# Retention and a gated feed-forward on one core: the first two batches of attention loaded with two tokens per partition and cut by head halves, the first down projection by rows

## The chip, the cores and the metric

The kernel runs on one core of a Trainium2 chip. The metric is the device time in microseconds (us) of one execution, as the median of the runs; three runs of the kernel before gave 305.97 us (305.95 to 306.12). The engines are named as the profile names them: PE (matmuls; its weight loads PEld), DVE, ACT, POOL, and SP, which here only issues DMAs. q1 is the queue of SP's DMAs.

## The reference

```
scores = q @ k^T / sqrt(64)             # 8 batches, 8 heads, 576 tokens, 64 per head
ret    = scores * gamma_h^(i - j) for i >= j, else 0      # gamma_h = 1 - 2^(-5-h)
x      = (ret @ v), heads side by side  # 4608 tokens x 512
h      = x @ w_in                       # 512 x 2048
out    = (h * sigmoid(beta * h)) @ w_out  # 2048 x 512, float32
```

The decay gamma^(i-j) is a product of a gain per query and a gain per key, so the kernel scales q by one (table gq) and v, or in one place k, by the other (table gv), and the rest is linear attention with a causal mask: within a chunk of 128 tokens the masked scores, and from earlier chunks a carried state k^T v per head.

## The kernel before

**Blocks.** 512 tokens of each batch form a block of four chunks of 128; the last 64 tokens of all eight batches form a ninth block, the tails. A block's attention gives xT (the 512 values of a token on partitions); `up` (L466) makes one of 16 slices `fo` of 128 hidden values for a block with four matmuls of 512 columns and a Silu on ACT; `down` (L499) adds the slices of a token group `ms` (a quarter of the block) into one bank and copies it out. Order of the blocks: 0 to 6, tails, 7.

**Order of the work.** Nothing is scheduled for the kernel: each engine runs its instructions in the order in which the program issues them. The opening (L540 to L589) is written out by hand: batch 0, chunk by chunk. Then `merged` (L526) walks through `fill`, the list of up and down pieces, and puts every step of `streams` whose key is at most n ahead of `fill[n]`. d0 is the index of the first down piece of block 0 in that list (16; 15 after the change, as the first half pair leaves the list), u1 that of the first up of block 1. The steps of batch 1's attention have keys from d0+7 to u1+7, so that they lie between downs of block 0 and ups of block 1.

**One chunk of batch 0 or 1.** Loads: q of a batch with four tokens per partition (runs of 1 KB, `load_q` L73), k and v by chunk with one token per partition (runs of 256 bytes, `load_kv` L85). `pre_q` and `pre` (L241, L255) scale and cast them to bf16; `t_q`, `t_k` (L297, L304) transpose on PE and copy out of PSUM on ACT or DVE; `a_sc` (L317) makes the scores of 8 heads into two banks, and DVE multiplies each with the mask (L332) into R; `a_st` (L389) adds the chunk to the state, and copies it into block-diagonal tiles sbds; `a_O` (L367) multiplies R with v, `a_cross` (L353) adds the carried state's part, `a_x` (L379) copies to xT. In the opening, 14 dummy matmuls of 128 columns (`warm_up`, L209) lie between these steps. From batch 2 on, transposes are DMAs and other functions are used (`a_O4`, `a_cross4`, `x4`).

**Weights.** w_in comes in eight pieces of 256 columns (512 KB each), cast to bf16 by POOL and DVE (L185, L188); w_out in four of 1 MB, cast and divided by beta on POOL, DVE and ACT (L200, L202, L204). All DMAs but one are issued by SP, in program order: q, k and v of batch 0, w_in, w_out, batch 1, batch 2. In up 1 the first 10 slices are made in two halves of 256 columns, chunks 0 and 1 first, so that they can start before chunks 2 and 3 are done.

PSUM has eight banks: three with the tag mm, two sc, two O, one st.

## Time and profile before

| | us |
|---|---|
| median of the runs | 305.97 |
| the profiled execution | 305.54 |
| its span | 303.8 |
| PE busy | 293.4 (97% of the span) |
| ACT, DVE, POOL busy | 134.1, 108.0, 99.9 |
| first up of block 0 (PE, L488) | 18.46 |
| first down of block 0 (PE, L506) | 32.96 |
| first up of block 1 | 51.11 |
| first down of block 1 | 68.01 |

The span is the time from the first to the last instruction in the profiled execution; the execution's own time has 1.74 us more around it. A row of an order of time gives start, length, engine, line, operation, out<-in, shapes, the count of merged instructions, and in brackets how long the engine stood before it and what released it. Matmuls overlap, so that the length of a PE row is some 0.16 us more than the distance to the next.

### The profile page before, as it was taken

To read this page: it belongs to the slowest core of one execution; us is meant where nothing else is said; L and a number is where in the kernel's file an instruction comes from. 1 tells how busy PE (TensorE), PEld (TensorE's weight loads), DVE (VectorE), ACT (ScalarE), POOL (GpSimd) and SP (SyncE) were. 2 spreads that over 40 slices of the span, in tenths; PEclk is the share of its full clock that TensorE was granted. 3 is DMA by queue.
4 is the path that set the end of the run, shared out by engine and by line. 5 is a ranking of instruction groups with operands and counts; after the bars stand their busy time and mean duration, and the time that the engine had idled before them with its cause. 6 is when DMAs were issued, how large, how long until landed. Compare 5 with 4: busy or idle time off the path is not lost.

```text
span 303.8 us, 5689 instructions
## 1 busy us (share of the span) xinstructions
PE 293.4 (97%) x2311; PEld 151.3 (50%) x2345; DVE 108.0 (36%) x202; ACT 134.1 (44%) x227; POOL 99.9 (33%) x138
## 2 busy tenths in 40 slices
PE   7799999999999999999999999999999999999995
PEld 5544456854544454445444544454455544444444
DVE  6588566504640433133222413151346510020012
ACT  5567546781147313741374127511771058107700
POOL 4666317552840723350308030942342000000000
PEclk9999999999999999999999999999999999999999
DMA  8999999999999999908982889997996110131011
GB/s 210 219 344 363 385 252 244 237 189 243 173 249 265 233 190 230 262 12 158 252 219 66 156 226 243 214 187 184 185 200 112 60 45 0 32 73 35 2 69 69
DMA packets 129210, 53.86 MB, mean 177 GB/s; under 512 B 109968, under 2 KB 122656, under 8 KB 129184
## 3 DMA queue, kind: packets, MB, share of 16 engines
q1 hardware_dynamic: 129152, 53.49, 78.4%
q8 instruction: 18, 0.29, 0.4%
q14 instruction: 8, 0.07, 0.1%
q10 hardware_dynamic: 32, 0.01, 0.0%
HBM read 36.71 MB, written 9.44 MB: 152 GB/s over the span
## 4 chain that ended last, share of the span: by engine, by line
PE 87%; DMA 6%; SPq 4%; issue 1%; POOL 1%; DVE 0%; POOLq 0%
PE po L506 41%; PE ph L473 36%; SPq L94 3%; DMA wt<-in_moe_w_out_dram 3%; PE sc L327 3%; DMA wt<-in_moe_w_in_dram 2%; PE O L441 2%; PE st L402 2%; PE O L453 1%; SPq L177 1%; POOL w_out_sb L200 1%; PE O L376 0%; PE st L405 0%; SPq L82 0%; PE T L307 0%
## 5 line engine op out<-in xcount | busy, mean ns | idle before, releaser
L475 ACT ACTIVATE gT<-ph,beta_sb 128x512 bf16<-128x512 f32 (+1 forms) x152 | 99.5, 659 | 82.2 <-PE ph L473 81.7
L506 PE MATMUL po<-w_out_sb,gT 128*128 128x512 bf16 (+2 forms) x591 | 127.1, 368 | 2.1 <-issue 1.3
L473 PE MATMUL ph<-xT,w_in_sb 128*128 128x512 bf16 (+1 forms) x592 | 125.1, 365 | 0.8 <-issue 0.2
L473 PEld LDWEIGHTS <-w_in_sb 128*128 128x128 bf16 x608 | 58.4, 98 | 63.0 <-DVE w_in_sb L188 0.9
L506 PEld LDWEIGHTS <-gT 128*128 128x128 bf16 x608 | 56.8, 98 | 63.9 <-issue 0.6
L332 DVE TENSOR_TENSOR R<-sc,causal 128x512 bf16<-128x512 f32 x72 | 45.0, 684 | 81.4 <-PE sc L327 80.3
L513 DVE COPY ot<-po 128x512 f32<-128x512 f32 (+2 forms) x34 | 22.4, 657 | 77.2 <-PE po L506 74.4
L277 POOL CAST kn<-kvn 128x512 bf16<-128x512 f32 x32 | 19.5, 612 | 55.5 <-DMA kvn<-in_k_dram 55.1
L259 POOL TENSOR_TENSOR vn<-kvn,gv 128x512 bf16<-128x512 f32 x32 | 33.3, 1042 | 13.1 <-DMA kvn<-in_v_dram 6.3
L251 POOL TENSOR_TENSOR qs<-qn,gq 128x512 bf16<-128x512 f32 x24 | 24.3, 1042 | 35.1 <-DMA qn<-in_q_dram 35.1
L408 ACT CAST sbq<-st 128x256 bf16<-128x256 f32 x18 | 6.6, 369 | 35.8 <-PE st L402 35.8
L461 DVE CAST xT<-O 128x512 bf16<-128x512 f32 x20 | 12.7, 685 | 20.2 <-PE O L453 20.2
L327 PE MATMUL sc<-qT,kT 64*128 64x128 bf16 x256 | 10.8, 218 | 0.7 <-ACT kT L308 0.6
L188 DVE CAST w_in_sb<-wt 64x256 bf16<-64x256 f32 x32 | 10.7, 334 | 1.4 <-DMA wt<-in_moe_w_in_dram 0.3
L461 ACT CAST xT<-O 128x512 bf16<-128x512 f32 x8 | 4.7, 587 | 13.4 <-PE O L453 13.4
L327 PEld LDWEIGHTS <-kT 64*128 64x128 bf16 x288 | 8.2, 94 | 3.8 <-issue 1.7
L185 POOL CAST w_in_sb<-wt 128x256 bf16<-128x256 f32 x16 | 7.2, 469 | 5.3 <-DMA wt<-in_moe_w_in_dram 5.3
L402 PEld LDWEIGHTS <-kn 128*64 128x64 bf16 x192 | 5.1, 110 | 7.6 <-issue 6.4
L212 PE MATMUL ph<-warm 128*128 128x128 f32 (+1 forms) x24 | 6.5, 405 | 1.2 <-DVE warm L119 1.2
L441 PE MATMUL O<-R,vn 128*64 128x128 bf16 x224 | 7.7, 220 | 0.0
L402 PE MATMUL st<-vn,kn 128*64 128x64 bf16 x192 | 7.4, 200 | 0.0
L266 POOL TENSOR_TENSOR kn<-tln,gq 128x512 bf16<-128x512 f32 x4 | 4.2, 1042 | 9.8 <-DMA tln<-in_q_dram 5.9
(69 smaller groups left out, 103.4 us busy)
## 6 DMA issues: line engine op xcount, KB each, us to landing
qn<-in_q_dram SPq DMA_DIRECT2D x16, 512.0 KB, 5.8
kvn<-in_k_dram SPq DMA_DIRECT2D x32, 256.0 KB, 5.1
kvn<-in_v_dram SPq DMA_DIRECT2D x32, 256.0 KB, 5.0
out_dram<-ot SPq DMA_DIRECT2D x31, 256.0 KB, 2.8
wt<-in_moe_w_out_dram SPq DMA_DIRECT2D x4, 1024.0 KB, 9.7
wt<-in_moe_w_in_dram SPq DMA_DIRECT2D x6, 512.0 KB, 8.6
out_dram<-ot SPq DMA_DIRECT2D x9, 128.0 KB, 2.4
wt<-in_moe_w_in_dram SPq DMA_DIRECT2D x4, 256.0 KB, 5.8
```

The lines of the kernel that those rows point to most:

```text
L251: e.tensor_tensor(batch[b]["qs"][:, cs, hs], q_tiles[b][:, hs, cs].rearrange("p h i d -> p i h d"), gq[:, cs, hs].unsqueeze(3).to_broadcas ...
L259: nc.gpsimd.tensor_tensor(live[i]["vn"][:], kv_tiles.pop(i)[:, 1], gains(gv, c), ALU.mult)
L277: nc.gpsimd.tensor_copy(kn[:, c % 2], t[:, 0])
L327: nc.tensor.matmul(view(sc[j][:, p, :]), L["kT"][r, p, :], rhs, start=True, stop=True, skip_group_check=True)
L332: nc.vector.tensor_tensor(R[:, j], sc[j][:], m_b, ALU.mult)
L402: nc.tensor.matmul(st[j * D:(j + 1) * D, p, :D], L["kn"][:, 2 * p + j, :], L["vn"][:, 2 * p + j, :], start=(c == 0 and p == 0), stop=True, ...
L441: nc.tensor.matmul(out4(i, p, hh), L["vn"][:, 2 * p + j, :], rhs if b is None else rhs.rearrange("k (i s) -> k i s", i=CB), start=c % 2 == ...
L461: (nc.scalar.copy if n == 1 else nc.vector.tensor_copy)(to, O.rearrange("k p i s -> k p (i s)") if b is None else O[:])
L473: nc.tensor.matmul(ph, w_in_sb[:, ko, fo * P:(fo + 1) * P], xts[m][:, ko, :, w], start=(ko == 0), stop=(ko == KO - 1))
L475: nc.scalar.activation(gts[m][:, fo, :, w], ph, ACT.Silu, scale=beta_sb[:, fo:fo + 1])
L506: nc.tensor.matmul(po[:, :nn], gT[:, fo, ms, :], w_out_sb[:, fo, n0:n0 + nn], start=(fo == 0), stop=(fo == FO - 1))
L513: (nc.scalar.copy if m == 0 else nc.vector.tensor_copy)(ot, po[:, :nn])
```

## The change

- Batches 0 and 1 are loaded in spans of 256 tokens with two neighbouring tokens on a partition, so that a run of k or v has 512 bytes (for batch 1, q too); batch 0 by halves of the heads, all keys first. A chunk is then one half of the partitions of a span.
- Batch 0 is computed by head halves. Its keys take the gain in place of its values. Scores, outputs, states and carried terms of both batches work on halves of the partitions; batch 1's carried term stays 128x128. Batch 1 adds up its states anew for each chunk from the spans. No dummy matmul stands between the opening's steps.
- The first up pair is split: its first half (xT of heads 0 to 3) stands before the xT copy of the other heads. Rows of w_in are ordered to suit (head pairs p//2 instead of p%2, also in `a_O4`, `a_cross4`, `x4`).
- Down of block 0 takes one row `fo` for all four token groups at a time; the fourth group uses the st bank. w_out is loaded in half pieces, batch 1's first span is loaded ahead of the last w_out piece, whose cast has the key d0+12. Up 1 is in halves throughout.
- Masks of later batches and the zeroes of sbds are made on POOL after w_in's casts; the safe betas are made on DVE.

The longest parts of the diff; what is not shown are the gain tables, new masks (`cuts`, one per token parity), tile shapes and the renamed halves of `up`.

```diff
+    def load_span(b, j, cc, hs):
+
+        if (b, j, cc) not in spans:
+            spans[b, j, cc] = stage.tile([P, H, 2, D], F32, name="kvn", tag="kvn", bufs=NQ)
+        nc.sync.dma_start(spans[b, j, cc][:, hs].rearrange("p h i d -> p h (i d)"),
+                          (k, v)[j][b, hs, cc * W:(cc + 1) * W, :].rearrange("h (p i) d -> p h (i d)", i=2))
...
+    for j, g in ((0, 0), (0, 1), (1, 0), (1, 1)):
+        for cc in range(2):
+            load_span(0, j, cc, both[g])
...
+        if g == 0:
+            nc.sync.dma_start(t[:, :2], w_in_r[:, :2, f0:f0 + fn])
+            for ko in (2, 3):
+                for a, b in ((0, D), (D, 0)):
+                    nc.sync.dma_start(t[a:a + D, ko], moe_w_in[ko * P + b:ko * P + b + D, f0:f0 + fn])
...
+        for ko in kos:
+            if ko < 2 or g == 0:
+                (nc.vector if ko == 3 else nc.gpsimd).tensor_copy(w_in_sb[:, ko, f0:f0 + fn], t[:, ko])
...
+        for w in range(0, KO, 2):
+            nc.sync.dma_start(t[:, w:w + 2], w_out_r[:, g * KO + w:g * KO + w + 2, :])
...
+            hs, cs, e = slice(n // 2 * HP, (n // 2 + 1) * HP), slice(n % 2 * 2, n % 2 * 2 + 2), (nc.vector, nc.gpsimd)[n % 2]
+        elif b == 1:
+            hs, cs, e = slice(n % 2 * HP, (n % 2 + 1) * HP), slice(n // 2 * 2, n // 2 * 2 + 2), nc.vector
...
+        gain = gq2 if b == 1 else gq
...
+    def pre_span(b, j, cc, hs, e, gain=False):
+
+        if (b, cc) not in pair:
+            pair[b, cc] = [sb.tile([P, 2, H, D], BF16, name="kn", tag="kn", bufs=4),
+                           sb.tile([P, 2, HP, P], BF16, name="kT", tag="kT", bufs=4),
+                           sb.tile([P, 2, H, D], BF16, name="vn", tag="vn", bufs=3)]
+        put(e, pair[b, cc][2 * j][:, :, hs], spans[b, j, cc][:, hs].rearrange("p h i d -> p i h d"),
+            gv2[:, 2 * cc:2 * cc + 2, hs].unsqueeze(3).to_broadcast([P, 2, hs.stop - hs.start, D]) if gain else None)
...
+    def t_k(b, cc, ps, tag, e):
+
+        kn, kT = pair[b, cc][:2]
+        T = psum.tile([P, 2, len(ps), P], BF16, name="T", tag=tag, bufs=BANKS[tag])
+        for i in range(2):
+            for n, p in enumerate(ps):
+                nc.tensor.transpose(T[:, i, n, :], heads(kn[:, i], p), ident[:])
+        evict(e, kT[:, :, ps[0]:ps[-1] + 1, :], T[:])
...
+    def sc_span(b, cc, g, tags):
+
+        kT = pair[b, cc][1]
+        Rs[b, cc, g] = R = sb.tile([P, 2, 2, 2, P], BF16, name="R", tag="R", bufs=4)
+        sc = [psum.tile([P, 2, 2, P], F32, name="sc", tag=tag, bufs=BANKS[tag]) for tag in tags]
+        for n, i in ((n, i) for n in range(2) for i in range(2)):
+            p = 2 * g + n
+            for j, h in ((0, 0), (1, 1), (0, 1), (1, 0)):
+                r = slice(j * D, (j + 1) * D)
+                nc.tensor.matmul(by(b, sc[j][h * D:(h + 1) * D, n, i, :]), kT[r, i, p, h * D:(h + 1) * D], q_span(b, 2 * cc + h, r, p),
+                                 start=True, stop=True, skip_group_check=True)
+        for j in range(2):
+            nc.vector.tensor_tensor(R[:, j], sc[j][:], cuts[b][:].unsqueeze(1).to_broadcast([P, 2, 2, P]), ALU.mult)
...
+    def O_span(b, cc, g):
+
+        vn, R = pair[b, cc][2], Rs[b, cc, g]
+        for n, i in ((n, i) for n in range(2) for i in range(2)):
+            p = 2 * g + n
+            for j, h in ((0, 0), (1, 1), (0, 1), (1, 0)):
+                r, hh = slice(h * D, (h + 1) * D), j ^ p // 2
+                key, o = region(b, 2 * cc + h, p)
+                nc.tensor.matmul(o[hh * D:(hh + 1) * D], vn[r, i, 2 * p + j, :], by(b, R[r, j, n, i, :]),
+                                 start=begins(key, (hh,)), stop=False, skip_group_check=True)
...
+    def cross_span(b, c, ps):
+
+        cc, h = (c - 1) // 2, (c - 1) % 2
+        for p in ps:
+            key, o = region(b, c, p)
+            if b:
+                nc.tensor.matmul(o, sbds[c - 1][:, 2 * p:2 * p + 2].rearrange("k h d -> k (h d)"),
+                                 q_span(b, c, slice(0, P), p), start=False, stop=True, skip_group_check=True)
+                continue
+            for j in range(2):
+                r, hh = slice(j * D, (j + 1) * D), j ^ p // 2
+                nc.tensor.matmul(o[hh * D:(hh + 1) * D], sbq[c - 1][r, p, :], q_span(b, c, r, p), start=False, stop=True,
+                                 skip_group_check=True)
...
+    def st_terms(b, x, ps, terms, at=0):
+
+        for p in ps:
+            for t, (d, r) in enumerate((d, r) for d, r in terms):
+                kn, _, vn = pair[b, d]
+                for i in range(2):
+                    for j in range(2):
+                        o = (*states[b], x, p, j)
+                        nc.tensor.matmul(states[b][0][j * D:(j + 1) * D, x, p, :], kn[r, i, 2 * p + j, :], vn[r, i, 2 * p + j, :],
+                                         start=begins(states[b][1], (j,)), stop=True, skip_group_check=True)
...
+    low, high, rows = slice(0, D), slice(D, P), slice(0, P)
+
+    def new_states(b, cc, tag):
+        states[b] = (psum.tile([P, 2, HP, D], F32, name="st", tag=tag, bufs=BANKS[tag]), ("st", b, cc))
+    def blocks_of(x, to, es):
+
+        for j in range(2):
+            r = slice(j * D, (j + 1) * D)
+            evict(es[j], to[r, slice(1, 7) if j else slice(0, 10)].rearrange("k (u y) d -> k u y d", u=2)[:, :, 0:3:2],
+                  states[1][0][r, x].rearrange("k (u y) d -> k u y d", u=2))
+    def st_early(b, ps, es):
+
+        st_terms(b, 0, ps, [(0, low)])
+        st_terms(b, 1, ps, [(0, rows)])
+        if b == 0:
+            evict(es[0], sbq_all[:, 0:2, ps[0]:ps[-1] + 1], states[b][0][:, :, ps[0]:ps[-1] + 1])
+        else:
+            for x in range(2):
+                blocks_of(x, sbds[x], es)
+    def st_late(b, ps, es):
+
+        st_terms(b, 1, ps, [(1, low)] if b == 0 else [(0, rows), (1, low)])
+        if b == 0:
+            evict(es[0], sbq[2][:, ps[0]:ps[-1] + 1], states[b][0][:, 1, ps[0]:ps[-1] + 1])
+        else:
+            blocks_of(1, sbds[2], es)
+    def st_end(b, e):
+
+        st_terms(b, 1, range(HP), [(1, high)])
+        evict(e, ends[b][:], states[b][0][:, 1])
+    def x_span(b, key, es):
+
+        for h, e in enumerate(es):
+            O = Os[b, key][h]
+            if b == 0:
+                evict(e, xt(b)[:, 2 * key:2 * key + 2].rearrange("k p i (c h s) -> k (p i) c h s", c=2, h=2)[:, :, :, h],
+                      O.rearrange("k p i c s -> k (p i) c s"))
+            else:
+                evict(e, xt(b)[:, :, 2 * key:2 * key + 2, h * D:(h + 1) * D], O[:])
...
-            pos_[ms] = psum.tile([P, d_model], F32, name="po", tag="mm", bufs=3)
+            tag = "st" if (m, ms) == (0, 3) else "mm"
+            pos_[ms] = psum.tile([P, d_model], F32, name="po", tag=tag, bufs=BANKS[tag])
...
+        (nc.scalar.copy if m == 0 and ms % 2 == 0 else nc.vector.tensor_copy)(ot, po[:, :nn])
...
+    V, A, Z = nc.vector, nc.scalar, nc.gpsimd
+
+    g0, g1, lo2, hi2 = both[0], both[1], (0, 1), (2, 3)
     betas()
     betas_safe()
...
+    warm_up(4)
+    pre_q(0, 0)
+    pre_q(0, 1)
+    t_q(0, 0, "mm", A)
+    pre_q(0, 2)
+    pre_q(0, 3)
+    t_q(0, 1, "mm", A)
+    pre_span(0, 0, 0, g0, V, True)
+    t_k(0, 0, lo2, "mm", V)
+    pre_span(0, 0, 1, g0, Z, True)
+    pre_span(0, 0, 0, g1, Z, True)
+    pre_span(0, 0, 1, g1, Z, True)
+    sc_span(0, 0, 0, ("sc", "sc"))
+    t_k(0, 1, lo2, "mm", A)
+    sc_span(0, 1, 0, ("O", "O"))
+    pre_span(0, 1, 0, g0, Z)
+    pre_span(0, 1, 1, g0, Z)
+    t_k(0, 0, hi2, "mm", A)
+    sc_span(0, 0, 1, ("sc", "sc"))
+    t_k(0, 1, hi2, "mm", A)
+    new_states(0, 0, "st")
+    st_early(0, lo2, (A,))
+    new_span_O(0, 0, ("O", "O"))
+    O_span(0, 0, 0)
+    sc_span(0, 1, 1, ("mm", "mm"))
+    pre_span(0, 1, 0, g1, Z)
+    pre_span(0, 1, 1, g1, Z)
+    O_span(0, 1, 0)
+    st_late(0, lo2, (A,))
+    for c in (3, 1, 2):
+        cross_span(0, c, lo2)
+    st_early(0, hi2, (A,))
+    new_span_O(0, 1, ("sc", "sc"))
+    O_span(0, 0, 1)
+    x_span(0, 0, (A, A))
+    cast_w_in(0, (0, 1))
+    O_span(0, 1, 1)
+    st_late(0, hi2, (A,))
+    for c in (3, 1, 2):
+        cross_span(0, c, hi2)
+    up_pair(0, 0, 0)
+    x_span(0, 1, (V, A))
+    cast_w_in(0, (2, 3))
     cast_w_in(1)
     nc.vector.reciprocal(rbeta_sb[:], beta_sb[:])
...
+    def masks():
+
+        nc.gpsimd.memset(causal2[:], 1.0)
+        nc.gpsimd.affine_select(out=causal2[:], in_=causal2[:], pattern=[[1, P]], compare_op=ALU.is_ge,
+                                fill=0.0, base=0, channel_multiplier=-1)
+        nc.gpsimd.memset(causal2[:TL, TL:], 0.0)
+        cut_of(1)
+        nc.gpsimd.memset(causal[:], 1.0)
+        nc.gpsimd.affine_select(out=causal[:], in_=causal[:], pattern=[[1, CB], [CB, PC]], compare_op=ALU.is_ge,
+                                fill=0.0, base=0, channel_multiplier=-1)
+        for t in sbds:
+            nc.gpsimd.memset(t[:], 0.0)
+
+    fill = [F(up_pair, 0, 0, 1)] + [F(up, 0, fo) for fo in range(2, FO)]
...
-    def down_rows(n):
-
-        for fo, ms in [(2 * n + x // 2, x % 2) for x in range(4)] if n < 2 else [(fo, 2) for fo in range(4)]:
+    def down_row(n):
+
+        for fo, ms in [(n, ms) for ms in range(4)] if n < FO - 2 else [(fo, 2 * (n - FO + 2) + x) for x in range(2) for fo in (FO - 2, FO - 1)]:
             down(0, ms, fo, 1)
 
-    fill += [F(down_rows, n) for n in range(3)]
-    fill += [F(down, 0, ms, f0) for f0 in range(4, FO, 4) for ms in range(3)]
-    fill += [F(down, 0, 3, f0) for f0 in range(0, FO, 4)]
+    fill += [F(down_row, n) for n in range(FO)]
...
     u1 = len(fill)
-    fill += [F(up, 1, fo, 2 * x, 2) for x in range(2) for fo in range(10)]
-    fill += [F(up, 1, fo) for fo in range(10, FO)]
+    NH = FO
+    fill += [F(up, 1, fo, 2 * x, 2) for x in range(2) for fo in range(NH)]
+    fill += [F(up, 1, fo) for fo in range(NH, FO)]
     fill += [F(down, 1, ms, f0) for ms in range(MB // P) for f0 in range(0, FO, 4)]
-    base = {1: u1 + 10}
...
+    def span_sc(cc, g):
+        sc_span(1, cc, g, ("O", "O") if g else ("sc", "sc"))
+
+    def span_out(cc, g):
+
+        if g == 0:
+            new_span_O(1, cc, ("sc", "sc"))
+        O_span(1, cc, g)
+
+    def span_st(cc):
+
+        new_states(1, cc, "st" if cc else "O")
+        (st_late if cc else st_early)(1, range(HP), (A, V))
+
+    def span_rest(cc):
+
+        if cc:
+            cross_span(1, 2, range(HP))
+        cross_span(1, 2 * cc + 1, range(HP))
+        x_span(1, cc, (A, V))
+
+    def kv1(cc, t):
+        return [(t, F(load_q, 1, (cc,)))] + [(t, F(load_span, 1, j, cc, all_h)) for j in range(2)]
+
+    def span_steps(cc, q0, tq, k0, tk, s0, v0, t0, o0, x0):
+
+        return [(q0, F(pre_q, 1, 2 * cc)), (q0, F(pre_q, 1, 2 * cc + 1)), (tq, F(t_q, 1, cc, "O", V)),
+                (k0, F(pre_span, 1, 0, cc, both[0], A)), (k0, F(pre_span, 1, 0, cc, both[1], Z)),
+                (tk, F(t_k, 1, cc, range(HP), "O", A)), (s0, F(span_sc, cc, 0)), (s0 + .01, F(span_sc, cc, 1)),
+                (v0, F(pre_span, 1, 1, cc, both[0], V, True)), (v0, F(pre_span, 1, 1, cc, both[1], Z, True)),
+                (t0, F(span_st, cc)), (o0, F(span_out, cc, 0)), (o0 + .01, F(span_out, cc, 1)),
+                (x0, F(span_rest, cc))]
...
+    streams = [[(0, F(st_end, 0, A)), (0, F(load_w_out, 0)), (0.1, F(cast_w_in, 2)), (2.1, F(cast_w_in, 3)), (2.2, F(load_w_out, 1)),
                 (4.1, F(cast_w_in, 4)), (6.1, F(cast_w_in, 5)), (6.2, F(load_w_out, 2)), (8.1, F(cast_w_in, 6)),
-                (10.1, F(cast_w_in, 7)), (10.2, F(load_w_out, 3))],
-               [(d0 - 4 + 3.3 * g, F(cast_w_out, g)) for g in range(WG)],
...
+                (10.1, F(cast_w_in, 7)), (10.5, F(masks))] + kv1(0, 10.15) + [(10.2, F(load_w_out, 3))] + kv1(1, 10.3),
+               [(d0 - 3 + 3 * g, F(cast_w_out, g)) for g in range(WG - 1)] + [(d0 + 12, F(cast_w_out, WG - 1))],
                [(10.4, F(load_q, 2))] + [(10.4, F(load_kv, 2 * CB + n)) for n in range(2)],
...
+               [(u1 + 5, F(load_kv, 2 * CB + 2)), (u1 + 8.1, F(x_q, XB, 0)), (u1 + 8.2, F(x_q, XB, 1)),
+                (u1 + 8.3, F(x_k, XB, 0)), (u1 + 8.5, F(load_kv, 2 * CB + 3)),
                 (base[2] - 4.5, F(release, 4)), (base[2] + 8, F(release, 4))],
...
+               [(u1 + 8, F(pre_q, XB, n)) for n in range(4)],
+               span_steps(0, d0 + 8.5, d0 + 9.5, d0 + 9.5, d0 + 10.5, d0 + 11.5, d0 + 12.5, d0 + 15.8, d0 + 15.9, u1),
+               span_steps(1, u1 + 1, u1 + 2, u1 + 3, u1 + 5, u1 + 8, u1 + 7, u1 + 11, u1 + NH - 1, u1 + NH),
+               [(u1 + NH + 2, F(st_end, 1, A))]]
```

## Prediction

> **What bounds the kernel now.** I read the busy time by stage first, then TensorE's waits, then its order of time. The columns of the first view are the stretch, its length, and busy time (count) of PE, PEld, DVE, ACT and POOL.
>
> ```profile
> 0.00:18.46 18.46, 14.08 (x149) 10.13 (x150) 11.03 (x29) 10.95 (x22) 10.21 (x26) 1.00 1.10 237
> 18.46:32.96 14.50, 14.25 (x62) 5.89 (x65) 11.74 (x35) 10.77 (x17) 8.38 (x19) 1.00 1.07 363
> 32.96:51.11 18.15, 17.89 (x135) 9.27 (x136) 10.87 (x20) 8.75 (x17) 6.25 (x8) 1.00 1.08 281
> 51.11:68.01 16.90, 16.83 (x156) 12.07 (x157) 5.38 (x10) 13.62 (x30) 10.77 (x12) 1.00 1.13 221
> 68.01:303.80 235.79, 230.35 (x1812) 113.96 (x1839) 69.00 (x110) 89.97 (x146) 64.33 (x74) 1.00 0.70 150
> ```
>
> From 18.46 us on PE is busy without a break, and the waits from 20 us to the end are nothing:
>
> ```profile
> PE po L506 <- issue: 1.3, 8, 0.2
> PE ph L473 <- issue: 0.2, 1, 0.2
> PE po L506 <- POOL w_out_sb L200: 0.2, 1, 0.2
> ```
>
> So the time is the opening (until the first up), plus PE's work, plus whatever waits a change puts in. Everything after up of batch 1 (68.01) keeps its instructions; only head pairs are regrouped there, at the same count and shape. The change is decided before 68 us. PE's order of time there:
>
> ```profile
> 18.46 0.59 PE L488 MATMUL ph<-xT,w_in_sb 128*128 128x512 bf16 x2 [0.17 <-ACT xT L386]
> 20.47 12.66 PE L473 MATMUL ph<-xT,w_in_sb 128*128 128x512 bf16 x55
> 32.96 1.55 PE L506 MATMUL po<-w_out_sb,gT 128*128 128x512 bf16 x6
> 34.66 9.22 PE L506 MATMUL po<-w_out_sb,gT 128*128 128x512 bf16 x41 [0.15 <-POOL w_out_sb L200]
> ```
>
> First up at 18.46, first down at 32.96. In the trace matmuls of 512 columns start 0.216 us apart, those of 256 0.109, those of 128 0.056.
>
> **The loads.** Each row below starts when its load lands (POOL, then DVE):
>
> ```profile
> 12.29 0.61 POOL L277 CAST kn<-kvn 128x512 bf16<-128x512 f32 x1 [0.16 <-DMA kvn<-in_k_dram]
> 13.47 0.61 POOL L277 CAST kn<-kvn 128x512 bf16<-128x512 f32 x1 [0.57 <-DMA kvn<-in_k_dram]
> 21.82 0.92 POOL L185 CAST w_in_sb<-wt 128x256 bf16<-128x256 f32 x2 [0.24 <-DMA wt<-in_moe_w_in_dram]
> 23.32 0.92 POOL L185 CAST w_in_sb<-wt 128x256 bf16<-128x256 f32 x2 [0.58 <-DMA wt<-in_moe_w_in_dram]
> 37.41 1.28 DVE L204 TENSOR_SCALAR w_out_sb<-wt,rbeta_sb 128x512 bf16<-128x512 f32 x3 [1.43 <-DMA wt<-in_moe_w_out_dram]
> 40.11 1.28 DVE L204 TENSOR_SCALAR w_out_sb<-wt,rbeta_sb 128x512 bf16<-128x512 f32 x3 [1.43 <-DMA wt<-in_moe_w_out_dram]
> ```
>
> 256 KB of keys in 256-byte runs take 1.18 us, 256 KB of w_in in 1 KB runs 0.75 (512 KB in 1.50), of w_out in 2 KB runs 0.68. Runs of 512 bytes are not in the trace: between 0.68 and 1.18; a straight line of the time per run through the first two gives 0.90, which I take. Eight loads of batch 0 then end at 6.2 (second half of q) + 7.2 = 13.4 instead of 15.8, and all weights come 2.4 us earlier. The three more issues for w_in's first piece (0.47 each on SP, by the chain of waits) lie under that backlog. (DMA: Bandwidth & Descriptors, Specifications, of the Trainium skill names 512 bytes as the smallest transfer at line rate; by that it would be 0.75 and 12.2 us. No run here shows it yet, and the opening below would gain at most 0.3 by it.)
>
> **The opening, step by step.** The safe betas move from POOL to DVE ahead of the first q product, and wait for ACT, which now has two more gain tables (0.2 each) before its table load: q products on DVE at 5.9 instead of 4.74. Two at 0.69 end at 7.2, the first key product at 7.9, transposes (0.4), DVE's copy (0.43) and scores (0.4) at 9.3. Eight mask products at 0.65 on DVE then end at 15.1, each pair also waiting for keys: POOL makes two q products and three key products at 1.04 (end 11.1), ACT copies four transposes at 0.58 (last 13.2). Behind them outputs, and on ACT in order: a state 0.4, two xT copies 0.59 (16.0 to 17.2), the last state 0.3 (17.5). PE's carried terms wait for that, so the first up pair starts at 17.95, 0.5 earlier. Its second half needs xT (18.8) and DVE's cast (19.2); st_end (0.45) lies in that wait. The long run of ups starts at 20.1 instead of 20.47 and, with weights early, runs 56 x 0.216 = 12.1 without its present 0.4 of stalls: first down at 32.2 instead of 32.96, **gain 0.8**. Ends: no gain, or 1.9 more if only loads set it. POOL's moved masks (seven memsets and four selects of 0.14 to 0.5 each by the nearest rows, 3.9 us) lie before its w_out casts at 1.26: row 1 of w_out at 33.0 against a need at 33.1, so nothing; 0.8 if they are at their upper end.
>
> **Batch 1, from first down to the end of up 1.** Before, 68.01 - 32.96 = 35.05 us, of which down 64 x 0.216 = 13.8 and up 13.9 leave 7.3 for attention. After, PE's own attention is 32 transposes 1.8; 64 scores and 64 outputs on 64x64 tiles, 0.056 per four as the trace's L453, 1.8; 12 carried terms 0.7; 80 state matmuls at 0.03 a pair as L402, 1.2; and 23 changes of tiling at 0.095 (first score of a group 0.15 behind a transpose, not 0.056), 2.2: 7.65. So +0.35. The waits are what costs:
>
> ```profile
> 47.32 2.59 DVE L332 TENSOR_TENSOR R<-sc,causal 128x512 bf16<-128x512 f32 x4 [0.94 <-PE sc L327]
> 44.41 1.02 ACT L302 COPY qT<-T 128x1024 bf16<-128x1024 bf16 x1
> 51.04 0.77 ACT L416 CAST sbd<-st 64x256 bf16<-64x256 f32 x2
> ```
>
> - **Row 12.** The cast of the last quarter of w_out is due at d0+12, just behind the scores of span 0 (d0+11.5), and just ahead of down_row(12), which reads its first row. Each engine runs in program order, so DVE does four mask products (2.59) before the cast (0.48). PE has 0.3 of scores left and then stands: 0.2 + 2.59 + 0.48 + 0.1 - 0.4 = 2.97. Today these casts are done at 41.4, long before the products at 47.3. The load is not the cause: w_out's last MB now follows 1.5 MB of batch 1 (5.4 us), lands its first half at 41.8, and PE comes to row 12 at 32.2 + 12 x 0.86 + 0.9 + 0.4 = 43.9. Ends: 2.5 and 3.7.
> - **Key copy.** Transposes at d0+11, scores one row (0.86) later, ACT's copy of 1024 columns 1.02 + 0.2: 0.4 (0 to 0.7).
> - **First half of up 1.** States, outputs, carried term and xT copies all stand at u1, directly ahead of the up that reads xT. After the carried term: 0.15 + 0.69 copy + 0.1, and ACT and DVE have last downs to copy first: 1.07 (0.5 to 1.3). Now one transpose group and a state lie in that gap.
> - **Second q.** Products (2 x 0.69) queue on DVE behind the xT copy, two half ups (0.87) hide less than they take: 0.4 (0 to 0.6).
> - **Second half.** The same shape at u1+16: 0.9 (0.5 to 1.2). Now three half ups (1.3) lie between.
>
> Sum 5.7 of waits, 0.35 of work: +6.1 (low ends 2.5 + 0.5 + 0.5 + 0.35 = 3.9); less the opening's 0.8: **+5.3**. ACT has 32 half silus at 0.43 per 0.437 of PE, and five more copies (2.9 us), but PE has 4.6 of attention there to let it catch up. SP's later transposes for batch 2 are issued behind POOL's products at some 57 us and needed after 73; PE shows no slack to absorb the delay later, nor waits that would grow. The profiled execution had a span of 303.8 and took 305.54, so 1.74 lies around it, and it was 0.43 below the median 305.97. Span 309.1, execution 310.8, on the median **311.3**.
>
> **Rivals.**
> - *The runs bring nothing* (512-byte runs at 1.18): values land at 15.7, POOL and ACT follow 1.1 later: 312.4. Chance 0.1.
> - *PE slower in the opening.* The dummy matmuls between attention steps go:
>
> ```profile
> L212 PE MATMUL ph<-warm 128*128 128x128 f32 x14 | 2.7, 297 | 0.0
> ```
>
>   The granted clock is 1.00 in every stretch above, with them. If it fell, the pair's eight matmuls (1.7) and the opening's groups in series (1.5) would take twice as long: +3.2, 314.5. Chance 0.1. (TensorE: Matmul & The Clock Gate of the Trainium skill, Part 1 and Part 4, says that an idle window halves the clock, and that transposes don't count as activity; no run here shows it.)
> - *The start follows the loads*, as now (last value 15.8, first up 18.46, 2.7 behind): 13.4 + 2.7 = 16.1, 1.9 better: 309.4. Chance 0.07.
> - *No wait at row 12*, were the cast ahead of the products: 308.3. Chance 0.06. Against it speaks the order in the code.
> - *Not slower.* The same start at the best rate: values at 6.2 + 8 x 0.68 = 11.6, first up at 14.3, 4.15 earlier and 0.4 of stalls gone: -4.55. It decides against the price of batch 1: at its central value 305.97 + 6.1 - 4.55 = 307.5, at its low ends 305.97 + 3.9 - 4.55 = 305.3. It needs these low ends and the first up before 15.0 us. DVE's and ACT's queues speak against it. Chance 0.07.
>
> **How the numbers follow.** The forecast has 0.60 and its own range, from the ends above, is 309.4 to 312.8. 0.2% (0.6 us) is about what a measurement of this kernel can tell from no change. The range 307.7 to 314.3 leaves out the last rival and part of the slower PE. Faster 0.05 and same 0.02 are the last rival; slower 0.93.
>
> **What would show it.** First up near 18.0 and first down near 32.2; key loads 0.9 apart; PE idle for about 3 us ahead of down_row(12), ended by DVE's w_out cast, with four mask products in front of it on DVE; two waits of about 1 us for xT; up 1 ending near 73.4. Wrong if PE stays busy between 32 and 73, or if the first up starts before 15.

## The result, and the profile after

The changed kernel takes **321.97 us** (median of 4 runs, 319.29 to 324.16) against 305.96 (305.95 to 306.12): ratio 1.0493, 95% interval 1.0426 to 1.0559. The slowest of the four, 324.16 us, lies over 1.5% above the fastest and is left out of the ratio. Slower, as forecast, but by 16 us where the forecast had 5.3. The profiled execution took 321.44 us with a span of 319.7. First the stages of the changed kernel, with the columns of the prediction's first table (stretch, length, busy time and count of PE, PEld, DVE, ACT, POOL; then granted clock, DMA share, GB/s):

```profile
0.00:21.23 21.23, 13.75 (x242) 10.29 (x242) 11.38 (x26) 9.56 (x20) 14.28 (x34) 0.84 1.01 285
21.23:36.45 15.22, 14.53 (x82) 6.41 (x81) 14.42 (x34) 11.12 (x17) 10.25 (x22) 1.00 1.02 337
36.45:60.52 24.07, 18.85 (x179) 9.25 (x179) 11.29 (x23) 6.57 (x12) 10.98 (x13) 0.93 1.13 274
60.52:82.94 22.42, 21.29 (x264) 16.77 (x265) 6.51 (x10) 16.11 (x36) 7.57 (x9) 0.92 0.82 154
82.94:319.70 236.76, 230.54 (x1813) 113.87 (x1839) 69.05 (x110) 90.02 (x146) 58.17 (x68) 1.00 0.61 138
```

The five stretches are longer by 2.77, 0.72, 5.92, 5.52 and 0.96 us. The column after POOL's count, the granted clock of PE, is the surprise: 1.00 in every row before, 0.84, 0.93 and 0.92 in three rows now. PE's waits (total, times, longest):

```profile
PE po L625 <- DVE w_out_sb L241: 2.8, 1, 2.8
PE ph L591 <- DVE xT L353: 2.0, 2, 1.2
PE sc L515 <- DMA kT<-kn: 1.0, 1, 1.0
PE ph L591 <- DVE w_in_sb L224: 0.6, 2, 0.3
```

Row 12's wait and the two for xT were forecast; the one on the tails' keys and those on w_in_sb were not. Now PE's order of time in batch 1:

```profile
48.61 0.64 PE L392 MATMUL sc<-qT,kT 64*64 64x128 bf16 x32 [0.24 <-ACT kT L353]
52.08 0.58 PE L625 MATMUL po<-w_out_sb,gT 128*128 128x512 bf16 x1 [2.82 <-DVE w_out_sb L241]
52.88 4.39 PE L625 MATMUL po<-w_out_sb,gT 128*128 128x512 bf16 x14 [0.22 <-issue]
57.20 0.81 PE L450 MATMUL st<-vn,kn 64*64 64x64 bf16 x32
...
60.52 1.05 PE L591 MATMUL ph<-xT,w_in_sb 128*128 128x256 bf16 x8 [1.19 <-DVE xT L353]
61.59 0.28 PE L360 MATMUL T<-ident,qs 128*128 128x128 bf16 x2
62.20 0.82 PE L360 MATMUL T<-ident,qs 128*128 128x128 bf16 x6 [0.32 <-DVE qs L287]
62.81 2.77 PE L591 MATMUL ph<-xT,w_in_sb 128*128 128x256 bf16 x12
```

After the wait, rows 12 to 15 take 52.08 to 57.20 = 5.12 us; 16 matmuls at 0.216 are 3.46. What follows this standstill is slow. PE's busy time and the granted clock (the number after POOL's count) in stretches of one clock window (3.4 us; between the groups rows are left out):

```profile
7.50:10.90 3.40, 1.50 (x26) 0.98 (x27) 2.73 (x3) 2.02 (x2) 3.10 (x4) 1.00 1.22 291
10.90:14.30 3.40, 2.13 (x40) 1.26 (x36) 2.38 (x4) 1.14 (x2) 3.10 (x5) 0.51 1.17 302
14.30:17.70 3.40, 3.31 (x92) 2.82 (x92) 1.86 (x4) 0.99 (x3) 1.84 (x5) 0.50 1.06 322
17.70:21.20 3.50, 2.49 (x90) 1.98 (x84) 0.91 (x2) 1.79 (x5) 1.12 (x4) 0.99 1.05 345
...
48.50:51.90 3.40, 0.64 (x32) 0.58 (x33) 2.75 (x5) 0.68 (x2) 1.35 (x2) 1.00 1.12 327
51.90:55.30 3.40, 3.00 (x7) 1.13 (x8) 1.51 (x4) 0.00 (x0) 2.42 (x3) 0.50 0.95 187
55.30:58.70 3.40, 3.29 (x73) 1.82 (x71) 1.63 (x3) 1.54 (x3) 3.40 (x6) 1.00 1.34 240
58.70:62.10 3.40, 1.73 (x14) 1.04 (x14) 2.94 (x5) 1.76 (x4) 2.29 (x3) 1.00 1.03 109
62.10:65.60 3.50, 3.40 (x21) 2.66 (x22) 1.33 (x3) 1.36 (x3) 0.00 (x0) 0.51 1.10 242
```

In these rows a stretch in which PE is busy for at most 2.1 of 3.4 us is followed by one at half clock, however busy that one is; behind 3.0 and 3.3 of 3.4 the clock is full again. Other traces show that the busy time alone doesn't decide it: behind 1.81 us (run 8, 35.1 to 38.5) and 1.64 (run 6, 232.4 to 235.8) the clock stayed full, and behind 3.05 (run 1, 16.7 to 20.1) it stayed at half. The halved stretches in this trace (10.9 to 17.8, 51.9 to 55.3, 62.1 to 65.6) are 3.4 us long or twice that. (The Trainium skill, TensorE: Matmul & The Clock Gate, Part 1, gives free-running windows of 3.41 us and two clocks; the trace agrees with both. It speaks of idle windows, of gaps of over 3.4 us and, for one kernel, of frequent short idles; here a wait of 2.82, and windows that were half busy, were enough.)

### The profile page after: what moved, and what is told of

Read it like the earlier page. It is cut to its first block, busy times and chain, and to the rows that moved or that the text cites. A ratio compares the mean times of both kernels' runs of the same rounds, so it can differ in the third digit from the quotient of the medians.

```text
span 319.7 us, 6204 instructions
## 1 busy us (share of the span) xinstructions
PE 299.0 (94%) x2572; PEld 156.6 (49%) x2605; DVE 112.7 (35%) x201; ACT 133.4 (42%) x228; POOL 101.3 (32%) x143
## 4 chain that ended last, share of the span: by engine, by line
PE 79%; DVE 2%; DMA 2%; issue 1%; ACT 0%
PE po L625 36%; PE ph L591 34%; PE sc L515 2%; PE O L560 2%; PE st L533 2%; DMA kT<-kn 2%; PE O L572 1%; PE st L450 1%; DVE qs L287 1%; DVE xT L353 0%; DVE R L395 0%; DVE sbd L353 0%; PE T L360 0%; ACT sbd L353 0%; PE O L423 0%
## 5 line engine op out<-in xcount | busy, mean ns | idle before, releaser
L591 PE MATMUL ph<-xT,w_in_sb 128*128 128x512 bf16 (+1 forms) x617 | 126.8, 360 | 3.2 <-DVE xT L353 2.0
L591 PEld LDWEIGHTS <-w_in_sb 128*128 128x128 bf16 x632 | 61.1, 99 | 64.0 <-DVE xT L353 2.3
L520 DVE TENSOR_TENSOR R<-sc,causal 128x512 bf16<-128x512 f32 x56 | 34.8, 683 | 74.5 <-PE sc L515 74.4
L287 POOL TENSOR_TENSOR qs<-qn,gq 128x512 bf16<-128x512 f32 x26 | 27.3, 1078 | 35.0 <-DMA qn<-in_q_dram 35.0
L311 POOL TENSOR_TENSOR vn<-kvn,gv 128x512 bf16<-128x512 f32 x24 | 25.0, 1044 | 23.0 <-issue 10.0
L332 POOL CAST kn<-kvn 128x512 bf16<-128x512 f32 x24 | 14.6, 612 | 49.1 <-DMA kvn<-in_k_dram 49.1
L395 DVE TENSOR_TENSOR R<-sc,cut 128x512 bf16<-128x512 f32 x16 | 10.1, 684 | 8.4 <-PE sc L392 8.4
L353 ACT COPY kT<-T 128x512 bf16<-128x512 bf16 (+1 forms) x5 | 3.8, 756 | 11.7 <-PE T L370 11.7
L515 PEld LDWEIGHTS <-kT 64*128 64x128 bf16 x224 | 6.3, 94 | 2.5 <-DMA kT<-kn 1.1
L515 PE MATMUL sc<-qT,kT 64*128 64x128 bf16 x192 | 7.4, 217 | 0.0
```

What stands on the lines that cost most here:

```text
L287: e.tensor_tensor(batch[b]["qs"][:, cs, hs], q_tiles[b][:, hs, cs].rearrange("p h i d -> p i h d"), gain[:, cs, hs].unsqueeze(3).to_broadc ...
L311: nc.gpsimd.tensor_tensor(live[i]["vn"], kv_tiles.pop(i)[:, 1], gains(gv, c), ALU.mult)
L332: nc.gpsimd.tensor_copy(kn[:, c % 2], t[:, 0])
L515: nc.tensor.matmul(view(sc[j][:, p, :]), L["kT"][r, p, :], rhs, start=True, stop=True, skip_group_check=True)
L520: nc.vector.tensor_tensor(R[:, j], sc[j][:], m_b, ALU.mult)
L591: nc.tensor.matmul(ph, w_in_sb[:, ko, fo * P:(fo + 1) * P], xts[m][:, ko, w], start=(ko == 0), stop=(ko == KO - 1))
```

## Experiments

Theory: the forecast waits are there, but each standstill also halves the clock of the next window; in the opening DVE and POOL slow each other; PE's own work in batch 1 is larger than I counted. Rivals: the time is the waits alone; the loads; the order of steps.

**1. The last cast ahead of the mask products.**
```
- (d0 + 12, F(cast_w_out, WG - 1))
+ (d0 + 11.2, F(cast_w_out, WG - 1))
```


> The changed kernel with one key altered: the cast of the last quarter of w_out stands ahead of span 0's mask products (key d0+11.2 instead of d0+12). Theory (the queue on DVE makes PE stand at row 12, and the standing makes the granted clock fall to half for the next 3.4 us): the 2.8 us wait before down_row(12) goes, the half clock from 51.9 to 55.3 us goes with it, which held the following 16 downs to 5.1 us instead of 3.5; so first down to the end of up 1 shrinks from 46.5 to 42.0 us, and the time from 322.0 to 317.5. Rival (the wait alone, the clock falls for some other reason): 2.8 us, 319.2, with a half clock still shown between 50 and 56 us. Rival (the load of the last quarter ends the wait): no change.

319.77 us, ratio 1.044 (1.0414 to 1.0466). The wait at row 12 and the half clock behind it are gone; first down to first down of block 1 falls from 46.49 to 42.45, near the theory's 42.0, and no halved stretch is left between 50 and 56 us, where the rival needed one. But the opening's half clock lasted 17 us in this execution (9.9 to 26.9, first down 39.35 instead of 36.45): the windows' grid lies elsewhere in each execution. So the whole gained only 2.2 where the theory had 4.5, and the place must be read, not the total.

**2. Small dummy matmuls in the opening** (13 of 128 columns, between the attention steps; each stands as two matmuls in the profile, so that the 14 of the kernel before are seven calls).


> The changed kernel with 13 dummy matmuls of 128 columns put back between the steps of the opening, into the bank that the states use later; 0.4 to 0.7 us each time where PE waits anyway. Theory (PE's few matmuls between 7.5 and 14.4 us make the clock fall): the granted clock stays 1.00 until the first up, and the first up comes 1.4 us earlier, at 19.8 instead of 21.2; the time falls by 1.4, to 320.5. Rival (the opening is held by POOL, DVE and ACT alone, the clock costs nothing): first up stays at 21.2. Rival (dummies delay real matmuls): first up later than 21.2.

319.71, ratio 1.0456 (1.0415 to 1.0497). From 7 us on the opening is at full clock, first up 19.08 instead of 21.23, first down 33.38 instead of 36.45. The row-12 wait was 3.57 here, and 6.8 us at half clock (48.0 to 54.8) began in it.

**3. The kernel before, without its seven 128-column dummy calls.**


> The kernel before without the seven calls of dummy matmuls of 128 columns between the steps of its opening (the five larger ones at the start stay). Theory (they keep the clock up): the granted clock falls to half somewhere between 7 and 18 us, the first up comes 1 to 2 us after 18.46, and the time rises from 306.0 to between 307 and 309. Rival (the dummies do nothing): 306.0, clock 1.00 throughout.

307.61, ratio 1.004 (1.002 to 1.0061): 10.2 us at half clock, first up 20.22 instead of 18.46. Those dummies carried the clock.

**4. POOL's masks and zero fills later** (key d0+9.6 instead of 10.5).


> The changed kernel with POOL's masks and zeroes moved from behind the last w_in cast (27.5 to 32.4 us) to behind the first key cast of batch 1 (key d0+9.6, some 40 us), where DVE has nothing to do. Theory (POOL's work beside DVE's w_in casts slows them from 0.29 to 0.43 us to 0.7 to 1.0 us and PE waits for the last ones): the casts stay under 0.5 us, PE's waits for w_in_sb (0.6 us) go, the first down comes 0.6 to 0.9 us earlier than 36.45; time 321.2. Rival (the slow casts come from POOL's w_out products, which read and are not moved): casts of 0.7 us and more remain, no change in time.

322.15, ratio 1.054 (1.049 to 1.0589): inconclusive in time (13.7 us of half clock in the opening). For the casts the group rows from 26.8 us on speak, changed kernel first, then this one:

```profile
L224 DVE CAST w_in_sb<-wt 64x256 bf16<-64x256 f32 x17 | 8.4, 493 | 0.4
```

```profile
L224 DVE CAST w_in_sb<-wt 64x256 bf16<-64x256 f32 x19 | 7.2, 380 | 0.4
```

Cast by cast, the changed kernel has three of 0.69 to 0.70 us beside POOL's zero fills of sbds (30.25 to 32.45 us) and two of 1.01 and 1.03 beside POOL's w_out products (32.43 to 34.54), where the others take 0.29 to 0.47. Here the three are gone, as the theory had it; two of 1.03 and 1.04 stay, beside the w_out products, as the rival had it. PE waits for w_in_sb no more; but it doesn't in run 2 either, with the masks in their old place, so that this wait needs the late opening too.

**5. Both covers** (1 and 2 together).


> The last cast ahead of the mask products, and small dummy matmuls in the opening, together (each alone gave some 2.2 us). Clock theory (each standstill of PE costs itself and a halved clock behind it, and the place of the halved stretch wandered in the single fixes): opening at full clock, first down at 33.4 as with the dummies alone, 19.6 us from there to the first up of block 1 as with the early cast alone, 22.4 from there to its first down (with the half-clock stretch behind the xT wait, 20.8 without it), 236.9 behind: 314.0 us, 312.4 without that stretch. More than either alone added up. Rival (the two gains are the waits alone and add up, or the time comes back behind them): 317.5 us or more.

315.81, ratio 1.0313 (1.0293 to 1.0334), against 314.0 by the theory and 317.5 by adding up: nearer to the theory. A new wait of 0.40 for POOL's w_out product came in. One half-clock window is left, 56.0 to 59.4, behind the xT wait (1.18) and the q wait (1.16).

**6. All covers**: also batch 1's steps earlier; not shown below are the moves of products and copies to POOL and ACT, and the banks of span 0's states and outputs.
```
- span_steps(0, ..., d0 + 11.5, d0 + 12.5, d0 + 15.8, d0 + 15.9, u1)
+ span_steps(0, ..., d0 + 11.2, d0 + 11.1, d0 + 13.1, d0 + 14.1, d0 + 14.2)
- span_steps(1, ..., u1 + 11, u1 + NH - 1, u1 + NH)
+ span_steps(1, ..., u1 + 11, u1 + 13, u1 + 14)
```


> As both covers, and the steps of batch 1 earlier: span 0's states ahead of row 14, its outputs, carried term and xT copies ahead of row 15, the value product of span 0 and the q products of span 1 on POOL, span 1's outputs and xT copies two half ups earlier. Nothing is left out. Clock theory: both xT waits (1.19 and 0.79) nearly gone, clock 1.00 from 20 us to the end, up 1 starts 17.3 to 18 us behind the first down, its first down 19.3 later: 308.6 us. What is left over before is then PE's own work in batch 1 (about 2.4 us by the starts of matmuls), 0.5 in the opening and 1.0 at the tails. Rival (ACT's and DVE's copies can't be hidden, PE waits at other places): 311 us or more, with waits of over 0.5 us in front of the carried terms or the outputs.

312.28, ratio 1.0186 (1.0141 to 1.0231). The theory had 308.6; the number lies in the rival's range, but without the waits in batch 1 that the rival needs. No wait for xT, and the view shows a clock of 1.00 throughout (though eight transposes take 0.99 us at 9.74, where 0.61 is usual: the matmuls still ran slow there). First down to first up of block 1 is 18.13, from there to its first down 19.61. In the profiled execution PE waited 4.17 us for the load of betas instead of 3.2, which delayed the opening (first up 20.53); the tails' wait was 2.0.

**7. No contention**: as 6, with betas_safe behind the opening's mask products and the masks at d0+4.


> As all covers, and the safe betas on DVE behind the mask products of the opening instead of ahead of its first q product, and POOL's masks and zero fills behind the casts of w_in (d0+4). Contention theory: DVE's casts of w_in stay at 0.29 to 0.45 us up to the last, the first key product ends at about 8.6 instead of 9.8, first up at 18.0 to 18.3 instead of 19.1, first down 1.0 to 1.3 earlier than with all covers: 307.4 us. Rival (ACT's state copies and not the products set the opening): first up stays at 19.0, 308.6 us, the casts of w_in short all the same.

310.06, ratio 1.0122 (1.0097 to 1.0146). The first key product ended at 8.62 instead of 9.81, but the first up came at 19.04. That is the rival's number, but the trace has another reason ahead of ACT's copies: the key product was ready, and PE had not got to it.

```profile
9.07 0.89 PE L669 MATMUL dm<-warm 128*128 128x128 f32 x6
9.79 0.39 PE L370 MATMUL T<-ident,kn 128*128 128x128 bf16 x4
```

PE came to the key transposes at 9.79, behind the q transposes and three dummies (six rows), and at 9.83 in run 2. So this run doesn't tell what an earlier key product is worth. The stages from first down on:

```profile
33.34:51.47 18.13, 17.36 (x179) 8.74 (x180) 11.44 (x18) 6.90 (x14) 10.20 (x16) 1.00 1.07 307
51.47:71.08 19.61, 19.41 (x265) 15.67 (x265) 6.15 (x9) 16.45 (x37) 10.85 (x12) 1.00 1.11 203
71.08:308.70 237.62, 230.53 (x1813) 113.94 (x1839) 69.10 (x110) 89.93 (x146) 62.63 (x72) 1.00 0.68 143
```

With no wait above 0.35 us left and the clock at 1.00, the two stretches of batch 1 last 37.74 us; before 35.05. Counted from start to start, 1.6 of these 2.7 us are attention (6.22 before, 7.81 here); the other 1.1 lie in the rows of ups and downs, with waits of 0.34, 0.24 and 0.20 us among them. The states, before and here:

```profile
L405 PE MATMUL st<-vn,kn 128*128 128x128 bf16 x16 | 1.6, 220 | 0.0
```

```profile
L450 PE MATMUL st<-vn,kn 64*64 64x64 bf16 x48 | 1.9, 198 | 0.0
L450 PE MATMUL st<-vn,kn 128*64 128x64 bf16 x32 | 1.4, 203 | 0.0
```

Counted from start to start, 16 matmuls of 128 columns take 0.90 us, the 80 small ones 1.46 + 1.10 = 2.56. Two of the small ones start together, 0.003 us apart, and the next two 0.028 later; but where the tiling changes the next start comes 0.12 to 0.13 later, and this stretch has 26 changes of tiling (12 before), 11 of them behind states.

**8. All four q products of batch 0 on DVE** (as 2, none on POOL).


> As the dummies in the opening alone, but all four q products of batch 0 on DVE, as in the kernel before, none on POOL. Contention theory: with POOL quiet each q product takes 0.69 us on DVE (1.07 beside POOL's 1.04 to 1.55), the four 2.8 in all; POOL's first key product starts when its keys land and takes 1.04 to 1.2. DVE's own key product, beside POOL's, still takes over 1.0. First up within 0.6 of the 19.1 with dummies alone, time 319 to 320.5. Rival (the products are slow for their data's layout, not for POOL): 1.0 us each on DVE, and the first key product ends at 11.5 or later.

318.89, ratio 1.0404 (1.038 to 1.0428). First up 18.85 (19.08 in run 2). DVE in the changed kernel, then here:

```profile
6.23 2.13 DVE L287 TENSOR_TENSOR qs<-qn,gq 128x512 bf16<-128x512 f32 x2
8.29 1.52 DVE L294 TENSOR_TENSOR kn<-kvn,gv 128x512 bf16<-128x512 f32 x1
```

```profile
5.86 2.49 DVE L287 TENSOR_TENSOR qs<-qn,gq 128x512 bf16<-128x512 f32 x4
8.27 0.69 DVE L294 TENSOR_TENSOR kn<-kvn,gv 128x512 bf16<-128x512 f32 x1
```

Single products take 0.69 on DVE and 1.04 on POOL alone. Where they meet, the one that started first keeps its time and the other pays: DVE behind POOL 1.52 and 1.53, POOL behind DVE 1.39 to 1.55 (1.13 and 1.15 where the DVE product was nearly done). Here DVE's key product started at 8.27, POOL's at 8.46: DVE 0.69, POOL 1.39. My expectation of over 1.0 for DVE was wrong for that reason. (The Trainium skill, SBUF — State Buffer, Who interferes with whom, says that a DVE instruction with two SBUF inputs contends with a POOL instruction that reads, and of shared-port modes that the first to issue blocks the other; the trace agrees.)

The profiled execution, at 322.02 us the slowest of the five, has a wait that the changed kernel hadn't:

```profile
36.70 7.93 PE L625 MATMUL po<-w_out_sb,gT 128*128 128x512 bf16 x35 [2.02 <-POOL w_out_sb L237]
```

The last piece of w_in landed at 29.35 us there (26.71 in the changed kernel's profile), POOL's masks and fills followed, and its w_out products only at 35.46. No halved clock followed this wait.

**9. Tuned**: as 7, q products on DVE, fewer dummies, the opening's last state copy on DVE, the first tails' transposes ahead of SP's last six tail loads, the safe betas behind w_in's first casts.


> As the run without contention, and: all q products of batch 0 on DVE, fewer dummy matmuls (each was seen to hold up the transposes behind it by 0.1 to 0.15 us), the last state copy of the opening on DVE, which idles there for 1.75 us, and the transposes of the first two tails ahead of SP's last six loads of tails instead of behind them (they waited some 4.9 us in SP's queue). Theory: first score at 9.8 to 10 instead of 10.7, first up at 17.6 to 18.3 instead of 19.0, and PE's wait at the tails (1.8 us in the profiled run, 0.9 to 2.0 in the others) gone: 307.6 us. What then stays over the kernel before is PE's own work in batch 1, 2.7 us between the first up of block 1 and its first down. Rival (the opening goes by ACT's chain of key and state copies, and the tail's wait is the latency of the queue): first up at 18.8 or later and a wait of 1 us at the tails, 309.5 us.

308.59, ratio 1.0085 (1.0049 to 1.0121), 1.0 over the theory. First up 18.68, no more than 0.4 gained there, with a wait of 0.69 that nothing releases. The tails' wait is gone: from first down of block 1 to the end 235.62, before 235.82. Scores of the tails in the changed kernel, then here:

```profile
243.95 0.43 PE L515 MATMUL sc<-kT 64*128 64x128 bf16 x8
245.36 0.40 PE L515 MATMUL sc<-kT 64*128 64x128 bf16 x8 [0.98 <-DMA kT<-kn]
```

```profile
232.25 0.66 PE L515 MATMUL sc<-kT 64*128 64x128 bf16 x16
```

**10. Batch 1 as in the kernel before**, opening as in 9.


> The opening of the tuned run (batch 0 by spans and head halves, dummies, late safe betas and masks), but batch 1 wholly as in the kernel before: four tokens per partition for q, keys and values in 256-byte runs, chunks of 128 tokens, states by 128x128 matmuls, its steps, its downs by twos and its half ups. Theory (the loss in batch 1 is PE's work on small tiles, +2.7 us, and not its loads): from first down to first down of block 1 35.1 us as before, against 37.7 in the run without contention; first up at 17.6 to 18.3 against 18.46, no wait at the tails: 305.4 us, a little under the kernel before. Rival (the loss is in the order of loads and steps that the first batch's change brings): 307 us or more, with waits of PE between 33 and 68 us.

306.19, ratio 1.0013 (0.999 to 1.0036): the time of before, where the theory had 305.4. Its stages from first down on:

```profile
33.33:51.07 17.74, 17.63 (x135) 9.28 (x135) 10.82 (x20) 8.63 (x17) 7.76 (x10) 1.00 1.10 278
51.07:67.97 16.90, 16.82 (x156) 12.03 (x157) 5.37 (x10) 13.62 (x30) 10.02 (x13) 1.00 1.03 220
```

34.64 us instead of 37.74 in run 9: without the spans of batch 1 the extra work is gone, and the span falls from 306.9 to 304.2. The opening had again a wait that nothing releases, 1.32 us:

```profile
16.98 0.41 PE L420 MATMUL O<-R,vn 64*64 64x128 bf16 x14 [1.32 <-issue]
```

**11. Safe betas in DVE's gap** (as 10).


> As the run with batch 1 as before, but the safe betas on DVE right behind the mask products of the opening, where DVE stood idle for 2.6 us, instead of between its first casts of w_in. In that run they held DVE 0.7 us ahead of the casts, PE waited 0.28 for w_in_sb and the stretch from first up to first down took 14.9 us against 14.3 in the runs with them elsewhere. Theory: that stretch back to 14.3, everything else as there: 305.6 us, 0.1% under the kernel before. Rival (the stretch is set by when w_in lands): 14.9 again and 306.2 us. If PE's wait at its 450th instruction (1.32 us there, released by nothing that the profile shows) is absent in the profiled execution, the first up comes at 17.2 instead of 18.4.

306.21, ratio 1.0018 (0.9992 to 1.0044). First up to first down is 14.30 again, so the betas had cost 0.6; but 7 of 12 executions lost it to a lower mean clock.

**12. More dummies** (as 11, with some of the dummies that 9 had taken out).
```
- warm_up(3) ... dummy(1) ... dummy(2) ... dummy(2)
+ warm_up(4) ... dummy(2) ... dummy(3) ... dummy(3)
```


> As the run before it, with one 256-column warm-up and three 128-column dummy matmuls more in the opening. That run's executions fell in two groups: five with a mean clock of 0.998 to 1.00 at 304.97 to 305.72 us, seven with 0.989 to 0.994 (one or two windows of 3.4 us at half clock) at 306.19 to 308.42. Clock theory: the two groups are one program whose opening fills the free-running windows barely enough; with more dummies nearly all executions are at 0.998 or more, median 305.2 to 305.7, under the kernel before (306.17 there) by 0.2 to 0.3%. The dummies' own cost is some 0.3 us. Rival (the half-clock windows lie elsewhere, or the dummies' delay costs as much as they save): the same two groups, median 306 us or more.

**305.48** us (305.07 to 306.17, 12 runs) against 306.20: ratio **0.9978** (0.9963 to 0.9993). All executions are at 0.998 or more. First up 17.70, first down 32.00 (18.46 and 32.96 before). In this one comparison it is 0.2% faster than the kernel before.

## Why the forecast had the direction and not the size

- **Loads: right.** Forecast 0.90 us per 256 KB in 512-byte runs; they landed at 7.07, 7.98, 8.88 and so on to 13.38, 0.90 apart, dearer than the 0.75 of 1 KB runs. The weights came 2.5 us earlier in this profile (last piece of w_in 26.71 instead of 29.25), but not in each execution (29.35 in run 8's).
- **Opening: wrong.** First up 21.23 instead of 17.95. A step that failed is "Two at 0.69 end at 7.2, the first key product at 7.9": it priced products by rows measured alone, and it ended at 9.81, since the second q product and the key product each met one of POOL that had started first; PE waited 0.83 for it. What that wait is worth by itself no run isolates: where the product came earlier (runs 7 and 8), dummies and transposes kept PE until 9.79 and 9.60. The larger part is the clock, which stood among the rivals at 0.1, with a price of 3.2: run 2 takes the half clock away, and first up is 19.08, first down 33.38. So 3.07 us of first down's delay of 3.49 go with the half clock: 2.15 by the first up, 0.92 behind it, where the waits for w_in_sb go too. The other 0.42 stand where the forecast had a gain of 0.8. Runs 9 to 12 brought the first up forward (18.68 to 17.70), with other queues changed as well. One part of the change the forecast doesn't price: the transpose of the betas now stands ahead of PE's warm-up matmuls, so that PE's first matmul waits for a load and comes at 3.22 us (1.24 before, 4.17 in run 6). No run took that back.
- **Masks on POOL, "so nothing; 0.8 at most": wrong.** In the changed kernel they delayed no w_out row; they slowed three of DVE's casts of w_in beside them (run 4), and PE waited 0.58 for the casts of that stretch. In runs 5 and 8, with the first down at 33.4 and 33.2 and w_in landing 1.6 and 2.6 us later, the place that the forecast named did count: PE waited 0.40 and 2.02 for POOL's w_out products behind the masks.
- **Waits of batch 1: right.** Row 12 was 2.82 (2.97 forecast), with exactly four mask products and the cast ahead of it; key copy 0.24 (0.4), first half 0.35 for sbd, whose copies on ACT and DVE came one behind the other (58.06, 58.46, 58.92, 59.32), and 1.19 for xT (1.07 for both), second q 0.32 (0.4), second half 0.79 (0.9). Sum 5.71, forecast 5.74.
- **PE's work in batch 1: the term "+0.35" was mis-sized.** With short waits it measured 2.7 (run 7 against before), 1.6 of it attention by starts. The error is in the working: the 7.3 for before was a remainder, and so held 1.1 us that the ups and downs take over 0.216 and 0.109 apiece; the 7.65 for after was a sum of attention alone, and near the 7.81 measured. Counted alike, attention goes from 6.22 to 7.81, nearly all by the states (+1.66). "80 state matmuls at 0.03 a pair" held; the states cost what they do by the changes of tiling between them, which the sum for after had (23 at 0.095; there are 26), and which it set against a remainder.
- **Clock in batch 1: missing.** The sum put it at nothing. Two halved windows at 1.66 and 1.65 us, 3.3 in all. The rival for a slower PE was confined to the opening, where dummies had been taken out; the waits that I forecast myself were enough to halve the clock behind them: without the wait at row 12 its halved stretch is gone (run 1), without those for xT the other (run 6).
- **After block 1's first down, "PE shows no slack ... nor waits that would grow": wrong by 1.0.** The tails' transposes landed later than their scores needed (the second of them landed 4.8 us behind its issue, 3.3 before). Run 9 shows that SP's order decides it; why the landing grew is open.

The sum for the profiled executions: opening 3.5 (3.1 of it gone with the half clock), waits of over 0.3 us in batch 1 5.5, clock there 3.3, work with short waits 2.7, tails 1.0: 16.0, of a measured 15.9. Of the rivals, "no wait at row 12" (308.3) was made in run 1 and came to 319.8: it took out that wait and left all else. "Not slower" needed the first up before 15.0; the best that any run reached is 17.70. Run 12's gain is its opening's: in its profile first down comes 0.96 earlier than before, and 0.63 of it is given back behind.

## What to carry to other kernels

Where a forecast has TensorE wait for some 1 us or more, give it a term for a half-clock window behind the wait (here 1.65 us each for two of them). It is a risk and not a fixed price: waits of 2.02 us (run 8) and 1.82 (run 7, at the tails) cost none. And look for dummy matmuls that a change takes out, as they may be what holds the clock. When two runs differ in the clock, compare stretches, not totals. Count attention work before and after in the same manner: both as sums by starts, or both as remainders.

## What the runs showed of the hardware

- The clock's windows lie differently in each execution (the halved stretch of the opening began at 10.9 us in the changed kernel's profile, at 9.9 in run 1's), and one program's times spread with what they halve: run 11's seven executions with a mean clock of 0.989 to 0.994 took 306.19 to 308.42 us, its five with 0.998 or more 304.97 to 305.72; run 12, with four more dummies and every mean clock at 0.998 or more, took 305.07 to 306.17.
- In five kernels (the changed one, runs 1, 9, 10 and 11) PE stood still for 0.25, 0.93, 0.69, 1.32 and 0.48 us before the same place in its stream, behind 450 matmuls and weight loads, whatever the instruction was; the kernel before reaches that count only at 35.5 us. Runs 2, 4 to 8 and 12 pass it without such a stop. What releases it the profile doesn't show, and no run tried it.
